# Attention with partitions as (key offset, head), column-tiled folds and v re-laid through DRAM, in a fused adaLN block

## The chip, the cores and the metric

The kernel runs on one core of one Trainium2 chip. The metric is the device time of one execution in microseconds (us). Engine names are those of the profile: PE is TensorE (matmul), PEld its weight loads, DVE VectorE, ACT ScalarE, POOL GpSimd, SP the engine whose queue issues nearly all the DMAs.

## The reference

One transformer block over 2048 rows of 512 columns: LayerNorm with modulation, sliding dilated attention, a residual, LayerNorm with modulation, a gated FFN, a residual. All in bf16.

```python
def _A_ref(x, wqkv, wo):                     # H = 32 heads of Dh = 16
    W, dil = (8, 2)                          # 8 keys per query: the positions s, s-2, ..., s-14
    qkv = ((x @ wqkv).reshape(B, S, 3, H, Dh)).transpose(2, 0, 3, 1, 4)
    ...
    logits = jnp.einsum('bhsd,bhswd->bhsw', q, kg) * scale      # masked where s - 2w < 0
    attn = _softmax(logits, axis=-1)
    o = jnp.einsum('bhsw,bhswd->bhsd', attn, vg)
    return o.transpose(0, 2, 1, 3).reshape(B, S, D) @ wo

def _B_ref(x, w_gate, w_up, w_down):         # Df = 1792
    return jnp.einsum('bsf,fd->bsd', _gelu(g) * u, w_down)

h = _layernorm(x) * (1 + ca) + sa            # sa..gb come from silu(c) @ w_mod
x = x + ga * _A_ref(h, A_wqkv, A_wo)
h = _layernorm(x) * (1 + cb) + sb
x = x + gb * _B_ref(h, B_w_gate, B_w_up, B_w_down)
```

## The kernel before

The rows are worked in four groups of 512 (`sg` 0 to 3). `qT`, `kT` and `vT` hold 128 partitions of (head, d4), four slices `j`, and 512 rows in the free dimension, so that a shift by a key offset is a shift in the free dimension. Feature d of a head is 4 d4 + j. `M` sums the four partitions of a head (column-tiled: four key offsets side by side in 32 PSUM partitions each). The softmax runs with rows on partitions, so there are transposes into it and out of it. P is then broadcast to the (head, d4) partitions through DRAM, and the sum over key offsets is done by PE, by multiplying with the identity and accumulating.

```python
def emit_attention(sg):
    qT, kT, vT = qkv_tiles[sg]
    for wg in range(2):
        LTp = psB.tile([P, SG], F32, name="LTp", tag="mm")
        # four products pq = qT * kT shifted by 2w, each 128x2048, on DVE   (cut)
        for j in range(4):
            for w4 in range(4):
                nc.tensor.matmul(LTp[32 * w4:32 * w4 + 32, :], lhsT=M[:], rhs=pqs[w4][:, j, :],
                                 start=(j == 0), stop=(j == 3), tile_position=(0, 32 * w4))
        nc.scalar.activation(out=LT[:, wg, :], in_=LTp[:], func=ACT.Identity, scale=DH ** -0.5)
    # LT -> transposes LNp -> max, subtract, Exp, sum, reciprocal, product -> transposes PTp -> PT   (cut)
    scr = dram.tile([P, 2, SG], BF16, name="scr")
    nc.sync.dma_start(out=scr[:], in_=PT[:])
    for w in range(W):
        wg, w4 = divmod(w, 4)
        pbc = pbcpool.tile([P, SG], BF16, name="pbc")
        src = bass.AP(scr.tensor, scr.offset + w4 * 32 * (2 * SG) + wg * SG, [[2 * SG, 32], [0, 4], [1, SG]])
        nc.sync.dma_start(out=pbc[:], in_=src)
    for jp in range(2):
        for w in range(W):
            pv = pvpool.tile([P, 2, SG], BF16, name="pv")
            nc.vector.tensor_tensor(out=pv[:], in0=_ap(pbcs[w][:], [[0, 2], [1, SG]]),
                                    in1=vT[:, 2 * jp:2 * jp + 2, 16 - 2 * w:16 - 2 * w + SG], op=ALU.mult)
            for i in range(2):
                nc.tensor.matmul(o_ps[i][:], lhsT=ident[:], rhs=pv[:, i, :], start=(w == 0), stop=(w == W - 1))
    # oT, x1 = x + oT @ (ga wo), LayerNorm 2 -> h2T   (cut)
...
for sg in range(NSG):
    emit_attention(sg)
    if sg == 0:
        emit_qkv(1); emit_ln1(2); emit_qkv(2); emit_ln1(3)
    elif sg == 1:
        emit_qkv(3)
    if sg >= 1:
        emit_ffn(sg - 1)
emit_ffn(NSG - 1, last=True)
```

## Time and profile before

| | before |
|---|---|
| time, median of the runs beside the changed kernel (range) | 306.0 us (305.72 to 306.5) |
| span of the profiled run, mean granted clock | 305.3 us, 0.993 |
| first FFN matmul of group 0 (g_ps) | 85.20 us |
| first LTp matmul of attention(2) | 143.90 us |
| first LTp matmul of attention(3) | 204.96 us (61.06 later) |
| from there to the end | 100.3 us |

The marks of the table are starts in PE's timeline. They cut the span into a front, one steady period (attention of one group woven with the FFN of the group before), and the rest.

From the profile's page of the kernel before: busy time, the 40 slices, and the chain of waits. Then two of its groups, in the form "line, engine, operation, tiles, shapes, count | busy us, mean ns of one | idle time before it".

```profile
PE 268.9 (88%) x1421; PEld 124.7 (41%) x1448; DVE 187.9 (62%) x344; ACT 150.5 (49%) x250; POOL 11.5 (4%) x21
...
PE   0699976899997999899968899899689998999995
PEclk9999999999999999999999999999979999999999
DMA  5999940401000401001000401110004000100001
...
PE 56%; DVE 10%; ACT 7%; issue 3%; DMA 2%; SPq 1%; POOL 1%; POOLq 0%; ACTq 0%; DVEq 0%
...
L308 DVE TENSOR_TENSOR pv<-pbc,vT 128x1024 bf16<-128x1024 bf16 x64 | 42.0, 689 | 4.1 <-DMA pbc<-scr 1.6
L248 DVE TENSOR_TENSOR pq<-qT,kT 128x2048 bf16<-128x2048 bf16 x32 | 37.7, 1217 | 3.7 <-ACT kT L230 3.0
```

The reader sees PE at 9 in most slices from the ninth on (61 us; a slice is 7.6 us), and at 56% of the chain: from about 60 us the time is PE's. The clock stands at full from 17.9 us on; before that the trace has no clock event, and the 9s of the first slices stand there for want of one. The pv products wait little (4.1 us in all, 1.6 of it for pbc).

From PE's timeline of the kernel before, in attention(2) ("start, us, engine line, tiles, count, idle before and what ended it"):

```profile
143.90 1.25 PE L252 MATMUL LTp<-pq,Mph 128*32 128x512 bf16 x17
...
157.42 1.02 PE L350 MATMUL u_ps<-h2T,Wu 128*128 128x512 bf16 x4 [1.55 <-ACT gl L353]
...
171.09 0.38 PE L311 MATMUL o_ps_1671<-pv,ident 128*128 128x512 bf16 x1
171.31 0.38 PE L346 MATMUL g_ps<-h2T,Wg 128*128 128x512 bf16 x1
```

The first line is where attention(2) begins. The next has one of the gaps that belong to the Exp and Gelu table loads on ACT (four loads of 1.28 us between 153.54 and 161.08). The last two show that a full matmul takes 0.216 us of PE's stream: read the distance of the starts, since the modelled 0.38 us overlaps.

### The profile page before, as it was taken

The page shows a single profiled execution, that of the slowest core. Times are in us where ns is not written, and L with a number is a line of the kernel's source. Part 1 is how long each engine was busy: PE and PEld are TensorE (multiplying, and loading weights), DVE is VectorE, ACT ScalarE, POOL GpSimd, SP SyncE. Part 2 cuts the span into 40 slices and gives each one's busy share as a digit, 9 for nine tenths or more (in the row PEclk, how much of TensorE's full clock was granted, in tenths as well). Part 3 has the DMA queues.
Part 4 walks back from the last instruction along what each step waited for, and adds up shares of the span by engine and source line. Part 5 has one row for each costly group of instructions (what it writes and reads, how often), then busy time and mean ns, then how long its engine had stood idle before and what let it go on. Part 6 is the DMA issues. An engine that isn't in the chain of part 4 may idle for free.

```text
span 305.3 us, 3861 instructions
## 1 busy us (share of the span) xinstructions
PE 268.9 (88%) x1421; PEld 124.7 (41%) x1448; DVE 187.9 (62%) x344; ACT 150.5 (49%) x250; POOL 11.5 (4%) x21
## 2 busy tenths in 40 slices
PE   0699976899997999899968899899689998999995
PEld 0445444444453444444323344443244444444442
DVE  4449889899887587522985597426456973222221
ACT  1258577436487543630597433305974343066600
POOL 1110100100200000100000000100000001000000
PEclk9999999999999999999999999999979999999999
DMA  5999940401000401001000401110004000100001
GB/s 175 364 401 344 333 124 34 137 0 54 17 2 0 151 22 38 33 17 37 17 1 34 141 0 53 34 37 17 0 34 140 0 17 19 37 16 2 0 33 35
DMA packets 19154, 22.53 MB, mean 74 GB/s; under 512 B 1856, under 2 KB 16960, under 8 KB 19136
## 3 DMA queue, kind: packets, MB, share of 16 engines
q1 hardware_dynamic: 19136, 22.29, 21.3%
q8 instruction: 11, 0.18, 0.2%
q14 instruction: 7, 0.06, 0.1%
HBM read 19.14 MB, written 3.15 MB: 73 GB/s over the span
## 4 chain that ended last, share of the span: by engine, by line
PE 56%; DVE 10%; ACT 7%; issue 3%; DMA 2%; SPq 1%; POOL 1%; POOLq 0%; ACTq 0%; DVEq 0%
PE u_ps L350 11%; PE y_ps L370 10%; PE g_ps L346 6%; PE qkv_ps L225 5%; PE y_psb L370 4%; PE g_psq L346 4%; PE LTp L252 3%; DVE x1b L326 2%; DVE st L109 2%; PE hTp L128 2%; ACT L276 2%; DMA pbc<-scr 1%; ACT ub L355 1%; DVE ssum L279 1%; PE x_ps L324 1%
## 5 line engine op out<-in xcount | busy, mean ns | idle before, releaser
L350 PE MATMUL u_ps<-h2T,Wu 128*128 128x512 bf16 x220 | 61.2, 383 | 6.5 <-ACT gl L353 6.2
L225 PE MATMUL qkv_ps<-hT,wqkv 128*128 128x512 bf16 x188 | 48.5, 393 | 4.5 <-DMA wqkv<-in_A_wqkv_dram 1.4
L357 DVE TENSOR_TENSOR hht<-gl,ub 128x512 bf16<-128x512 bf16 x56 | 23.4, 421 | 47.1 <-ACT ub L355 47.1
L346 PE MATMUL g_ps<-h2T,Wg 128*128 128x512 bf16 x161 | 47.4, 382 | 3.1 <-ACT ub L355 2.8
L355 ACT CAST ub<-u_ps 128x512 bf16<-128x512 f32 x56 | 32.8, 586 | 25.2 <-PE u_ps L350 25.0
L308 DVE TENSOR_TENSOR pv<-pbc,vT 128x1024 bf16<-128x1024 bf16 x64 | 42.0, 689 | 4.1 <-DMA pbc<-scr 1.6
L248 DVE TENSOR_TENSOR pq<-qT,kT 128x2048 bf16<-128x2048 bf16 x32 | 37.7, 1217 | 3.7 <-ACT kT L230 3.0
L353 ACT ACTIVATE gl<-g_ps 128x512 bf16<-128x512 f32 x42 | 25.3, 603 | 28.8 <-PE g_ps L346 28.1
L370 PE MATMUL y_ps<-WdP,hht 128*128 128x512 bf16 x164 | 37.6, 379 | 0.2
L350 PEld LDWEIGHTS <-Wu 128*128 128x128 bf16 x224 | 21.6, 98 | 32.9 <-issue 9.4
L346 PEld LDWEIGHTS <-Wg 128*128 128x128 bf16 x224 | 21.7, 98 | 28.4 <-issue 5.2
L225 PEld LDWEIGHTS <-wqkv 128*128 128x128 bf16 x192 | 21.3, 116 | 25.9 <-issue 8.2
L370 PEld LDWEIGHTS <-hht 128*128 128x128 bf16 x224 | 21.7, 98 | 24.8
L373 DVE TENSOR_TENSOR ot<-y_ps,x1b 128x512 bf16<-128x512 f32 x12 | 8.3, 692 | 25.4 <-PE y_ps L370 23.1
L311 PEld LDWEIGHTS <-ident 128*128 128x128 bf16 x128 | 12.3, 96 | 20.7 <-issue 9.9
L113 POOL TENSOR_TENSOR rstd<-rstd,neghalf 128x4 f32<-128x4 f32 x8 | 9.8, 1228 | 241.5 <-DVE rstd L112 241.5
L135 ACT ACTIVATE h2T<-hTp,modT,scl 128x512 bf16<-128x512 bf16 x16 | 11.6, 778 | 11.3 <-PE hTp L128 11.3
L254 ACT ACTIVATE LT<-LTp 128x512 f32<-128x512 f32 x8 | 4.8, 601 | 22.3 <-PE LTp L252 22.3
L324 PE MATMUL x_ps<-woP,oT 128*128 128x512 bf16 x63 | 15.5, 378 | 0.2
L346 PE MATMUL g_psq<-h2T,Wg 128*128 128x512 bf16 x55 | 14.3, 379 | 0.1
L228 ACT CAST qT<-qkv_ps 128x512 bf16<-128x512 f32 x16 | 9.4, 586 | 9.1 <-PE qkv_ps L225 9.0
L252 PE MATMUL LTp<-pq,Mph 128*32 128x512 bf16 x128 | 13.4, 383 | 0.0
(118 smaller groups left out, 275.1 us busy)
## 6 DMA issues: line engine op xcount, KB each, us to landing
pbc<-scr SPq DMA_DIRECT2D x32, 128.0 KB, 2.5
wm<-in_w_mod_dram SPq DMA_DIRECT2D x6, 512.0 KB, 6.6
x_sg<-in_A_x_dram SPq DMA_DIRECT2D x4, 512.0 KB, 4.1
xr<-in_A_x_dram SPq DMA_DIRECT2D x16, 128.0 KB, 2.0
out_dram<-ot SPq DMA_DIRECT2D x16, 128.0 KB, 1.7
Wg<-in_B_w_gate_dram SPq DMA_DIRECT2D x1, 1792.0 KB, 12.1
Wu<-in_B_w_up_dram SPq DMA_DIRECT2D x1, 1792.0 KB, 9.7
WdP<-in_B_w_down_dram SPq DMA_DIRECT2D x1, 1792.0 KB, 9.8
```

The source lines that it names most:

```text
L225: nc.tensor.matmul(ps[:], lhsT=wqkv[:, dt, blk * D + j:(blk + 1) * D:4], rhs=hT[:, dt, :], start=(dt == 0), stop=(dt == DT - 1))
L248: nc.vector.tensor_tensor(out=pq[:], in0=qT[:], in1=kT[:, :, 16 - 2 * w:16 - 2 * w + SG], op=ALU.mult)
L252: nc.tensor.matmul(LTp[32 * w4:32 * w4 + 32, :], lhsT=M[:], rhs=pqs[w4][:, j, :], start=(j == 0), stop=(j == 3), tile_position=(0, 32 * w4))
L308: nc.vector.tensor_tensor(out=pv[:], in0=_ap(pbcs[w][:], [[0, 2], [1, SG]]), in1=vT[:, 2 * jp:2 * jp + 2, 16 - 2 * w:16 - 2 * w + SG], op= ...
L311: nc.tensor.matmul(o_ps[i][:], lhsT=ident[:], rhs=pv[:, i, :], start=(w == 0), stop=(w == W - 1))
L324: nc.tensor.matmul(x1_ps[:], lhsT=oT[:, j, c4 * P:(c4 + 1) * P], rhs=woP[:, j, :], start=(j == 0), stop=(j == 3))
L346: nc.tensor.matmul(g_ps[:], lhsT=Wg[:, dt, ft * P:(ft + 1) * P], rhs=h2T[:, dt, :], start=(dt == 0), stop=(dt == DT - 1))
L350: nc.tensor.matmul(u_ps[:], lhsT=Wu[:, dt, ft * P:(ft + 1) * P], rhs=h2T[:, dt, :], start=(dt == 0), stop=(dt == DT - 1))
L353: nc.scalar.activation(out=gl[:], in_=g_ps[:], func=ACT.Gelu_apprx_tanh)
L355: nc.scalar.copy(out=ub[:], in_=u_ps[:])
L357: nc.vector.tensor_tensor(out=hht[:], in0=gl[:], in1=ub[:], op=ALU.mult)
L370: nc.tensor.matmul(y_ps[:], lhsT=hh[ft][:, c4 * P:(c4 + 1) * P], rhs=WdP[:, ft, :], start=(ft == 0), stop=(ft == FT - 1))
```

## The change

Its intent: spend fewer PE columns and less DVE time on attention. The partitions become (key offset r, head). The logits stay there, so no transposes are needed: the maximum is three DVE operations and a matmul that subtracts it in PSUM, the sums are column-tiled matmuls. The fold of pv over the four key offsets in the partitions becomes a 32-column matmul, four of them side by side (`tile_position`), instead of full matmuls with the identity. For that, v must lie in (r, head) partitions, each r shifted by two rows; it is written to DRAM and read back in that layout. x stays in SBUF instead of being read again, 14 dummy matmuls run at the start to wake PE's clock, and loads are issued in order of use. The `emit_` calls keep their order in the source, but the scheduled order of instructions changes: qkv(2) begins at about 50 us in the trace of the kernel before, and behind the start of FFN(0) in the changed kernel.

```diff
+        order = [(b, j) for j in range(4) for b in range(2)] + [(2, j) for j in range(4)]
         ...
+        scr = dram.tile([P, 4, HALO + SG], BF16, name="scr")
+        nc.sync.dma_start(out=scr[:], in_=vT[:])
+        row = HALO + SG
+        for j in range(4):
+            vRj = vrpool.tile([P, 4, VW], BF16, name="vR")                 # VW = 520
+            src = bass.AP(scr.tensor, scr.offset + 2 + j * row, [[2, 4], [16 * row, H], [4 * row, 4], [1, VW]])
+            nc.sync.dma_start(out=vRj[:], in_=src)
     ... (softmax: LNp, PTp, PT, pbc go; m3, NB, ss, rB come; cut)
-            for w in range(W):
-                nc.vector.tensor_tensor(out=pv[:], in0=_ap(pbcs[w][:], [[0, 2], [1, SG]]), in1=vT[...], op=ALU.mult)
-                for i in range(2):
-                    nc.tensor.matmul(o_ps[i][:], lhsT=ident[:], rhs=pv[:, i, :], start=(w == 0), stop=(w == W - 1))
+            for wg in range(2):
+                nc.vector.tensor_tensor(out=pv[:], in0=_ap(e[:, wg, :], [[0, 4], [1, SG]]),
+                                        in1=vR[j][:, :, 8 - 8 * wg:8 - 8 * wg + SG], op=ALU.mult)
+                for d4 in range(4):
+                    nc.tensor.matmul(o_ps[32 * d4:32 * d4 + 32, :], lhsT=F1[:], rhs=pv[:, d4, :],
+                                     start=(wg == 0), stop=(wg == 1), tile_position=(0, 32 * d4))
     ...
-    nc.sync.dma_start(out=woP[:], in_=A_wo.rearrange("(p j) n -> p j n", j=4))
+    nc.sync.dma_start(out=woP[:], in_=bass.AP(A_wo.tensor, A_wo.offset, [[4 * D, 4], [16 * D, H], [D, 4], [1, D]]))
+    for i in range(14):
+        nc.tensor.matmul(wps[:], lhsT=warm[:, 0:P], rhs=warm[:], start=True, stop=True)
```

## The prediction

> **What bounds it now.** TensorE, by its in-order stream, from about 60 us on. The page gives PE 268.9 us busy of 305.3, DVE 187.9, ACT 150.5. PE holds 56% of the chain of waits. The timeline shows full-size matmuls back to back every 0.216 us; counting by that spacing, real PE work is about 253 us. The rest: head 13.2 us to the first qkv matmul, about ten qkv matmuls at 0.43 us instead of 0.216 (13.2 to 17.8 us), tail 3.6 us after the last matmul, and PE idle in the middle. The timeline from one attention to the next (143.97 to 205.03) has 61 us for 52 us of PE work; its gaps are waits for ScalarE near the two Exp table loads (1.55, 1.39, 0.89), for P (0.5), for the P broadcast through DRAM (1.46) and for LN2 (1.14).
>
> **What the change does.**
> PE: o_ps falls from 128 full matmuls (27.6 us) to 128 32-column ones, four side by side. The LTp runs show 17 of these in 1.19 us and 13 in 0.97, so 0.054 each plus a fixed cost; a lone LTp costs 0.42 in all instead of 0.216. I read a fixed 0.3 to 0.36 us per group, which agrees with the Trainium skill, "TensorEngine Tiling (Array Packing)", Key Properties: changing the tiling mode drains TensorE. The new order alternates four folds with three or four FFN matmuls, so a group costs an estimated 0.58 us, not 0.22: 32 o_ps groups 14 to 18 us, and more LTp groups too. Gone: LNp and PTp transposes (5.5 us). New: max subtraction, sums, 1/sum broadcast, about 5 us. Net PE work down only about 8 to 12 us.
> DVE: mx, LT, ssum, rinv, e products (27.2 us) become three max, rinv, two copies and one product (about 15); pv 42.0 to 39 us; pq unchanged, 1.22 us each.
> ACT: PT copy (4.0) and one of two Exp table pairs per attention (2.6) go.
> DMA: P's round trip (2.0 plus 4.4 us in the chain) leaves the critical path; v's, four times larger, starts right after qkv and should be hidden.
> Head: 14 dummy matmuls should make the first qkv matmuls run at 0.216: 2 us.
>
> **How much is critical.** In the two steady periods I expect 55 to 57 us instead of 61: about 10 us. In the front the gain is nearly lost: attention(0) ends some 15 us earlier, but the new order puts LN1(2), LN1(3), qkv(2), qkv(3) after FFN(0) has begun, so PE has nothing to do while the DVE chain softmax, 8 pv, x1, LN2 runs (about 35 to 64 us, some 15 us idle). FFN(0) starts near 65 instead of 82 us. Front gain: 2 to 5 us.
>
> **Prediction: 290 us, 280 to 300 (8 in 10); faster by over 2%: 0.88, within 2%: 0.11, slower: 0.01.**
>
> **What shows it.** First qkv matmuls 0.216 us apart by 13 us; o_ps groups of four taking 0.5 to 0.6 us between FFN matmuls (0.3 would refute the mode-switch cost); pv 1.22 us; no wait on vR; PE share low between 35 and 65 us; distance between the LT runs of attention(2) and (3) 55 to 57 us; one Exp table load per attention.
>
> **What would make it wrong.** Switch cost hidden by queued weights: 280 or lower. pq with the overlapping key window or pv falling to half rate (2.2 us): slower, near 306. vR landing late beside Wu and WdP. Longer PE gaps in the front.

## The result

All ratios below are the mean time of one kernel's runs over that of the other's runs of the same rounds, so they are not quite the ratio of the medians quoted beside them. Executions over 1.5% slower than the fastest of the same kernel are left out of the means.

| | before | after |
|---|---|---|
| time, median (range) | 306.0 us (305.72 to 306.5) | 303.73 us (303.34 to 304.89) |
| ratio, 95% interval | | 0.9926 (0.9904 to 0.9947) |
| span of the profiled run, mean granted clock | 305.3 us, 0.993 | 302.1 us, 0.932 |
| first g_ps of FFN(0) | 85.20 | 83.09 |
| first LT matmul of attention(2) | 143.90 | 158.19 (14.3 later) |
| to the first LT matmul of attention(3) | 61.06 | 51.88 (9.2 less) |
| from there to the end | 100.3 | 92.0 (8.3 less) |

The kernel is 0.7% faster, within 2%; the forecast was 5%. The three stages add up: 14.3 - 9.2 - 8.3 = -3.2 us, the difference of the two spans. The two later stages gained more than was forecast. The front lost 14.3 us where a gain of 2 to 5 was forecast. The page of the changed kernel, in the same order:

```profile
PE 264.5 (88%) x1476; PEld 113.3 (38%) x1476; DVE 172.9 (57%) x305; ACT 142.0 (47%) x238; POOL 18.1 (6%) x41
...
PE   7696986128399999998999899899989989999995
PEclk9699899555669999999999999999999999999999
DMA  7999422694222122231220012100000000100000
...
PE 65%; DMA 12%; DVE 11%; SPq 4%; ACT 3%; POOL 2%; issue 1%; POOLq 0%; DVEq 0%; ACTq 0%
...
L318 DVE TENSOR_TENSOR pv<-e,vR 128x2048 bf16<-128x2048 bf16 x32 | 37.0, 1219 | 11.7 <-DMA vR<-scr 11.6
L273 DVE TENSOR_TENSOR pq<-qT,kT 128x2048 bf16<-128x2048 bf16 x32 | 37.9, 1212 | 6.4 <-PE LT_471 L276 6.4
```

Three things are new. PE's row falls to 1, 2, 8, 3 in slices 8 to 11 (53 to 83 us), with PEclk at 5 and 6 there. DMA holds 12% of the chain. The pv group now waits 11.6 us for vR, though one pv product takes the 1.22 us that was forecast.

DVE's timeline of the changed kernel in attention(0):

```profile
46.24 2.36 DVE L318 TENSOR_TENSOR pv<-e,vR 128x2048 bf16<-128x2048 bf16 x2
50.25 2.40 DVE L318 TENSOR_TENSOR pv<-e,vR 128x2048 bf16<-128x2048 bf16 x2 [1.65 <-DMA vR<-scr]
56.53 2.36 DVE L318 TENSOR_TENSOR pv<-e,vR 128x2048 bf16<-128x2048 bf16 x2 [3.88 <-DMA vR<-scr]
64.94 2.36 DVE L318 TENSOR_TENSOR pv<-e,vR 128x2048 bf16<-128x2048 bf16 x2 [6.05 <-DMA vR<-scr]
```

Four pairs of products take 9.5 us; they spread over 21 us, because each of the last three pairs waits for its load of v (1.65, 3.88 and 6.05 us). Next, the DMA issues on SP's queue, and the two pieces of the chain of waits that lie ahead of those products:

```profile
34.70 15.51 SPq L258 DMA_DIRECT2D vR<-scr  x4
50.25 5.68 SPq L389 DMA_DIRECT2D Wu<-in_B_w_up_dram  x1
55.97 1.34 SPq L390 DMA_DIRECT2D WdP<-in_B_w_down_dram  x1
```

```profile
25.36 9.28 DMA scr<-vT
...
44.51 20.31 DMA vR<-scr
```

The write of v to DRAM takes 9.3 us. SP then spends 15.5 us on issuing four loads; Wu and WdP, the FFN's weights, stand behind them in the queue. The last piece of the chain lasts 20.3 us, until the last of the four loads lands at 64.8 us. What the DMA engines did meanwhile is in the windows (columns: window and its length, busy us and count of PE, PEld, DVE, ACT, POOL, then granted clock, busy share of the 16 DMA engines, GB/s):

```profile
40.00:45.00 5.00, 3.90 (x30) 2.05 (x29) 1.49 (x4) 3.92 (x6) 0.00 (x0) 1.00 0.27 87
45.00:50.00 5.00, 4.74 (x26) 1.98 (x25) 3.57 (x3) 3.06 (x6) 0.23 (x1) 1.00 0.27 92
50.00:55.00 5.00, 0.80 (x8) 0.20 (x7) 2.40 (x2) 1.00 (x2) 1.04 (x1) 0.87 0.27 92
55.00:60.00 5.00, 1.23 (x8) 0.23 (x8) 2.36 (x2) 0.39 (x1) 0.00 (x0) 0.50 0.76 190
60.00:65.00 5.00, 0.00 (x0) 0.00 (x0) 0.06 (x1) 0.20 (x1) 0.00 (x0) 0.50 1.03 266
```

From 35 to 55 us the share is 0.27 and stays there: 4.3 engines' worth of 16, moving about 90 GB/s. Wu cannot be the competitor, since its issue began at 50.25 us. After that the share goes to 1.03. So the loads are slow because they do not use the engines, and not because the engines are busy. The single DMA packets in the kept trace show the same: the 1040-byte pieces of vR take 48 ns each, with 4.3 packets in flight on average from 34.7 to 56 us. The first three loads' pieces are through at 54.75 us, before the share rises. The fourth load's take 8.9 us instead of 5.8: some 3 us of the last wait of 6.05 come from sharing with Wu and WdP, by this estimate.

Last, PE's timeline of the changed kernel: the start of attention(2), against 143.90 before, and the fold in the steady part:

```profile
158.19 0.40 PE L276 MATMUL LT_1543<-pq,Mph 128*32 128x512 bf16 x4
...
177.43 0.59 PE L346 MATMUL g_ps<-h2T,Wg 128*128 128x512 bf16 x2
177.96 0.40 PE L321 MATMUL o_ps<-pv,F_157 128*32 128x512 bf16 x4
178.29 0.60 PE L346 MATMUL g_ps<-h2T,Wg 128*128 128x512 bf16 x2
```

Two g_ps matmuls should take 2 x 0.216 = 0.43 us; the group of four folds starts 0.53 us after them and takes 0.33 us itself. A group thus costs 0.43 us, not the 0.58 that was forecast (the median of the 15 such groups between FFN matmuls after 100 us is 0.43 too, the longest 0.48).

### The profile page after: what moved, and what is told of

It is laid out like the page before. It is cut to its first block, busy times and chain, and to the rows that moved or that the text cites. A ratio compares the mean times of both kernels' runs of the same rounds, so it can differ in the third digit from the quotient of the medians.

```text
span 302.1 us, 3849 instructions
## 1 busy us (share of the span) xinstructions
PE 264.5 (88%) x1476; PEld 113.3 (38%) x1476; DVE 172.9 (57%) x305; ACT 142.0 (47%) x238; POOL 18.1 (6%) x41
## 4 chain that ended last, share of the span: by engine, by line
PE 65%; DMA 12%; DVE 11%; SPq 4%; ACT 3%; POOL 2%; issue 1%; POOLq 0%; DVEq 0%; ACTq 0%
PE u_ps L350 13%; PE y_ps L368 12%; PE qkv_ps L246 10%; PE g_ps L346 9%; DMA vR<-scr 7%; PE y_psb L368 4%; PE g_psq L346 4%; PE x_ps L329 4%; SPq L258 3%; PE o_ps L321 3%; DMA scr<-vT 3%; DVE st L183 3%; PE hTp L200 3%; DVE x_sg L331 2%; DMA wm<-in_w_mod_dram 2%; POOL rstd L187 2%
## 5 line engine op out<-in xcount | busy, mean ns | idle before, releaser
L350 PE MATMUL u_ps<-h2T,Wu 128*128 128x512 bf16 x224 | 62.6, 383 | 0.0
L346 PE MATMUL g_ps<-h2T,Wg 128*128 128x512 bf16 x168 | 49.3, 387 | 0.9 <-ACT h2T L207 0.9
L318 DVE TENSOR_TENSOR pv<-e,vR 128x2048 bf16<-128x2048 bf16 x32 | 37.0, 1219 | 11.7 <-DMA vR<-scr 11.6
L350 PEld LDWEIGHTS <-Wu 128*128 128x128 bf16 x224 | 20.7, 98 | 25.5 <-issue 5.1
L321 PE MATMUL o_ps<-pv,F_157 128*32 128x512 bf16 x128 | 13.7, 416 | 14.5 <-DVE pv L318 14.4
L371 DVE TENSOR_TENSOR ot<-y_ps,x_sg 128x512 bf16<-128x512 f32 x12 | 8.3, 691 | 26.2 <-PE y_ps L368 21.6
L183 DVE BATCH_NORM_STATS2 st<-x_sg 128x6 f32<-128x512 bf16 x32 | 20.9, 672 | 3.8 <-DMA x_sg<-in_A_x_dram 3.8
L187 POOL TENSOR_TENSOR rstd<-rstd,neghalf 128x4 f32<-128x4 f32 x8 | 10.6, 1330 | 187.6 <-DVE rstd L186 187.6
L323 ACT CAST oT<-o_ps 128x512 bf16<-128x512 f32 x16 | 9.4, 586 | 23.2 <-PE o_ps L321 23.2
L329 PE MATMUL x_ps<-woP,oT 128*128 128x512 bf16 x64 | 18.8, 434 | 0.7 <-ACT oT L323 0.7
L207 ACT ACTIVATE h2T<-hTp,modT,scl 128x512 bf16<-128x512 bf16 x16 | 11.6, 787 | 14.7 <-PE hTp L200 14.6
L353 ACT ACTIVATE gl<-g_psq 128x512 bf16<-128x512 f32 x14 | 8.4, 597 | 14.6 <-PE g_psq L346 14.6
```

The lines of the kernel that those rows point to most:

```text
L183: nc.vector.bn_stats(out=st[:, c4, :], in_=xt[:, c4, :])
L318: nc.vector.tensor_tensor(out=pv[:], in0=_ap(e[:, wg, :], [[0, 4], [1, SG]]), in1=vR[j][:, :, 8 - 8 * wg:8 - 8 * wg + SG], op=ALU.mult)
L321: nc.tensor.matmul(o_ps[32 * d4:32 * d4 + 32, :], lhsT=F1[:], rhs=pv[:, d4, :], start=(wg == 0), stop=(wg == 1), tile_position=(0, 32 * d4))
L329: nc.tensor.matmul(x1_ps[:], lhsT=oT[:, j, c4 * P:(c4 + 1) * P], rhs=woP[:, j, :], start=(j == 0), stop=(j == 3))
L346: nc.tensor.matmul(g_ps[:], lhsT=Wg[:, dt, ft * P:(ft + 1) * P], rhs=h2T[:, dt, :], start=(dt == 0), stop=(dt == DT - 1))
L350: nc.tensor.matmul(u_ps[:], lhsT=Wu[:, dt, ft * P:(ft + 1) * P], rhs=h2T[:, dt, :], start=(dt == 0), stop=(dt == DT - 1))
```

## The experiments

Two theories were put against each other. Theory A: vR's source pattern has the key offset, a dimension of four, outermost, so each load runs on only four of the 16 DMA engines. The Trainium skill, "DMA: Bandwidth & Descriptors", section "Why a DMA increments its semaphore by 16 and not by 1", says that the number of engines is the largest k up to 16 that divides the slowest dimension (not of size 1) of both access patterns; the share of 0.27 agrees with k = 4. Theory B: the loads are slow for another reason (their size, 1040-byte pieces, the wait for the write to DRAM before them, or Wu and WdP beside them), or the front is lost to PE's clock or to the column-tiled matmuls. All kernels gave correct results. The changed kernel itself was not run again in the later batches, whose runs of the kernel before have medians of 306.44 to 307.87 us instead of 306.0. Differences from 303.73 below are therefore between batches; by the ratios they would be 1 to 1.5 us larger.

### Split vR's load so that heads are outermost (e1_vr16)

```diff
-            src = bass.AP(scr.tensor, scr.offset + 2 + j * row, [[2, 4], [16 * row, H], [4 * row, 4], [1, VW]])
-            nc.sync.dma_start(out=vRj[:], in_=src)
+            for r in range(4):
+                src = bass.AP(scr.tensor, scr.offset + 2 + j * row + 2 * r, [[16 * row, H], [4 * row, 4], [1, VW]])
+                nc.sync.dma_start(out=vRj[32 * r:32 * r + 32], in_=src)
```

> Only the load of vR changes: each of the 4 loads per group of rows is issued as 4 loads of 32 partitions, so that the outermost dimension of the read is 32 (heads) instead of 4 (key offsets). Same bytes, same pieces of 1040 B, same place in the queue. Theory A (a read whose outermost dimension is 4 runs on only 4 of the 16 DMA engines: share 0.27, 92 GB/s, 5.8 us per 520 KB): the waits of pv on vR fall from 11.6 us to under 2, the first g_ps starts at 65 to 70 us instead of 83, the DMA share is near 1 while vR lands, and the time is 284 to 290 us instead of 303.7. Rival B (small scattered pieces of 1040 B, or a DRAM write followed by a read, are slow in themselves) and rival C (vR is late because Wu and WdP compete with it): pv still waits 8 us or more and the time stays over 298 us. Rival D (the gain is eaten by the tiling-mode switches on TensorE or by the colder clock for its own reasons): vR lands early and the time still stays over 298 us.

Measured: 290.61 us (290.21 to 291.41), ratio to the kernel before 0.9461 (0.9421 to 0.9501). No pv product waits for vR. The first g_ps comes at 70.78 us instead of 83.09, attention(2) at 145.30 instead of 158.19. One of its windows:

```profile
40.00:45.00 5.00, 3.88 (x25) 1.71 (x25) 1.48 (x3) 4.28 (x7) 0.00 (x0) 1.00 0.69 195
```

The share goes from 0.27 to 0.69, and the same bytes flow twice as fast. In the packets, a piece of 1040 bytes still takes 47 ns, but 11 are in flight on average from 40 to 46 us. The 16 loads are issued in 10.85 us, 0.68 each, and their pieces move in 11.2 us, so probably the issuing bounds them now; no run tests that. About 13 us came back. The edit changes two things, the outermost dimension and the number of loads; the control below parts them. The time is just above the 284 to 290 expected.

### The control: split it as finely, with the key offset still outermost (e2_vr_split_k4)

```diff
+            for d4 in range(4):
+                src = bass.AP(scr.tensor, scr.offset + 2 + j * row + 4 * d4 * row, [[2, 4], [16 * row, H], [1, VW]])
+                nc.sync.dma_start(out=vRj[:, d4, :], in_=src)
```

> Control for the run before it: vR also loaded by 16 smaller loads instead of 4, of the same pieces, but split over the depth group, so that each still has the key offset (4) outermost. Theory A: nothing gained, pv waits 10 to 14 us for vR, DMA share 0.27 while vR lands, time 301 to 307 us. If splitting into more and smaller transfers is what helps (pipelining, or shorter queues), it lands with the run before it, under 292 us.

Measured: 301.33 us (300.83 to 302.33), ratio 0.981 (0.9767 to 0.9853), inside what theory A expected. The order of instructions on PE, DVE, ACT and SP is that of the changed kernel, but for the number of loads (in e1_vr16 the scheduler also moved some instructions on PE, DVE and ACT); the number and size of the loads are those of e1_vr16.

```profile
40.00:45.00 5.00, 3.88 (x25) 1.72 (x25) 1.48 (x3) 4.27 (x7) 0.00 (x0) 1.00 0.27 90
45.00:50.00 5.00, 4.95 (x33) 2.46 (x32) 4.31 (x4) 2.63 (x6) 0.24 (x1) 1.00 0.27 90
```

The share is 0.27 again (4.3 packets in flight), and pv waits 8.9 us for vR, a little less than the 10 to 14 expected. So it is the outermost dimension and not the size or number of the loads: 10.7 us between e2 and e1, which ran in the same batch. Splitting by itself is worth some 2 us (303.73 against 301.33, between batches); finer overlap with the products would explain it, but that was not tested.

### Split the wo load alone, and both loads (e3_wo16, e4_both16)

wo's new load also has a dimension of four outermost, `[[4*D,4],[16*D,H],[D,4],[1,D]]`.

```diff
+    for d4 in range(4):
+        nc.sync.dma_start(out=woP[32 * d4:32 * d4 + 32],
+                          in_=bass.AP(A_wo.tensor, A_wo.offset + 4 * d4 * D, [[16 * D, H], [D, 4], [1, D]]))
```

> Only the load of woP changes, the other load whose outermost dimension is 4: split in 4 loads of 32 partitions. Theory A says that it clogs 4 of the 16 engines, and that the loads behind it (wm block 3, Wg) finish late: the first LT matmul, held by wm block 3 until 29.05 us, should start near 26 us, and about 3 us be gained in all if vR moves up as much (299 to 302 us). If the load of woP has slack: 303 to 305 us. It may not be read as cleanly as the others, as the scheduler then also puts Wg behind vR in the queue.

Measured: 300.44 to 301.62 us in three runs (a fourth, 311.8, was slow and is left out), ratio 0.9791 (0.9743 to 0.984). vR's first load is issued at 29.6 us instead of 34.70, and pv still waits 11.5 us for vR. The kernel starts its v loads earlier and is held by them as before. The scheduler also moved Wg's load behind vR's here, so this run does not show how the gain divides between the two. The write of v and the start of its loads are what moved: 3.2 us from the issue of the one to the issue of the other (26.42 to 29.61), against 9.3 (25.36 to 34.70).

> Both loads split over heads. Theory A: the gain of vR alone plus up to 3 us: 281 to 288 us; TensorE still has an idle stretch before the first g_ps (softmax, pv, x1, LN2 on DVE with nothing else to do), of about 10 us, and with it a stretch at half clock. Rivals B, C: over 298 us.

Measured: 288.79 us (287.33 to 289.73), 0.8 us above what was expected, ratio 0.9387 (0.9331 to 0.9442); first g_ps at 69.08, attention(2) at 142.97, then 52.4 us to attention(3) and 92.2 to the end. DVE's timeline of it shows the eight products of attention(0) in one run, without a wait:

```profile
44.49 9.21 DVE L319 TENSOR_TENSOR pv<-e,vR 128x2048 bf16<-128x2048 bf16 x8
```

The two patterns together cost the changed kernel 15 us (303.73 against 288.79); in this the split into more loads and Wg's place behind vR, which moved here too, are included. What is left of the front's gain is 0.9 us (142.97 against 143.90). e9_both16_again is the same kernel in a later batch, as the base for the runs of that batch (the expectation speaks of another chip; the record lists chip 1 for both, so only the batch is known to differ):

> The kernel with both split loads once more, as the base of the three runs that share its chip (the first run of it was on another chip, with the kernel before 0.5% slower there). 287.5 to 289.5 us.

Measured: 288.74 us (287.48 to 289.9), ratio 0.9424 (0.9381 to 0.9468); attention(2) at 141.13.

### The changed kernel without its 14 dummy matmuls (e5_after_nowarm)

```diff
-    for i in range(14):
-        nc.tensor.matmul(wps[:], lhsT=warm[:, 0:P], rhs=warm[:], start=True, stop=True)
```

> The kernel after without its 14 dummy matmuls. The prediction counted 2 us for them. The trace of after shows the first qkv matmuls at half clock all the same (record 0.50 between 10 and 15 us; 48 matmuls in 12.7 us, as before), so the theory now is that the clock falls back between the dummies' end at 6.7 us and the first qkv matmul at 12 us, and that they are worth nothing: 303.5 to 304.5 us, within 0.5 us of after. If they do help, it is slower by 1 to 2 us.

Measured: 304.13 us (303.46 to 307.51), ratio 0.9934 (0.9892 to 0.9976), against 0.9926 for the changed kernel: the dummies are worth nothing that five rounds can see. PE's timeline of the changed kernel, and its windows, show why:

```profile
1.29 5.45 PE L154 MATMUL warm_ps<-warm 128*128 128x512 bf16 x14 [1.29 <-DVE neghalf L113]
...
11.96 8.39 PE L246 MATMUL qkv_ps<-hT,wqkv 128*128 128x512 bf16 x28 [1.30 <-DVE hT L204]
```

```profile
8.00:10.00 2.00, 1.39 (x28) 1.39 (x29) 1.31 (x4) 0.24 (x2) 1.03 (x4) 0.83 1.08 380
14.00:16.00 2.00, 2.00 (x6) 0.64 (x5) 2.00 (x6) 0.73 (x2) 0.00 (x0) 0.50 1.09 386
```

The dummies end at about 6.7 us; the first eleven of them start 0.43 us apart, the last ones 0.216, so they do wake the clock, at 5.9 us. Five microseconds of small matmuls and gaps follow, and the clock's record falls to 0.50 at 9.31 us. qkv starts at half rate all the same: its matmuls start 0.43 us apart until 16.0 us. The 48 matmuls of qkv(0) end at 24.7 us. In e5 they begin at 12.39 and end at 24.2. The Trainium skill, "TensorE: Matmul & The Clock Gate", section "What's actually happening", gives an idle window of about 3.4 us after which the clock halves. The record of this trace agrees in the length: full clock from 5.90 to 9.31 us, 3.41 us. But PE was not wholly idle in it (the last dummies and 32 matmuls of one column fall into it), so what counts as idle isn't shown here. In the kernel before, the trace has no clock event ahead of 17.90 us; its qkv matmuls start 0.43 us apart until 17.87 and 0.216 after. The dummies warmed the clock too early.

### The fold without column tiling (e6_fullfold)

e4_both16, with the four 32-column folds replaced by four full matmuls with zero-padded weights that accumulate in one PSUM tile.

```diff
-                    nc.tensor.matmul(o_ps[32 * d4:32 * d4 + 32, :], lhsT=F1[:], rhs=pv[:, d4, :],
-                                     start=(wg == 0), stop=(wg == 1), tile_position=(0, 32 * d4))
+                    nc.tensor.matmul(o_ps[:], lhsT=FD[:, d4, :], rhs=pv[:, d4, :],
+                                     start=(wg == 0 and d4 == 0), stop=(wg == 1 and d4 == 3))
```

> On top of both split loads: the fold of pv into o_ps by full 128x128 matmuls with zero-padded weights (as many as the change has, 128, each 0.216 us, no change of tiling mode) in place of four 32-column ones side by side. The trace of after shows a group of four at 0.33 us plus about 0.1 us before it (0.43), against 4 x 0.216 = 0.86 for full ones, so the column tiling saves 0.43 us a group, 14 us of TensorE time in 32 groups. If TensorE is the limit there: 10 to 14 us slower than the kernel with both loads split (299 to 303 us). If the pace of pv on DVE (1.22 us a group) sets the time: under 4 us slower.

Measured: 302.22 us (301.67 to 303.06), ratio 0.9857 (0.9816 to 0.9898). PE's timeline of it:

```profile
167.95 1.02 PE L326 MATMUL o_ps<-pv,FD 128*128 128x512 bf16 x4
168.81 0.38 PE L355 MATMUL u_ps<-h2T,Wu 128*128 128x512 bf16 x1
```

A group of four takes 0.86 us, against 0.43 for the tiled one. Over 32 groups that is 32 x 0.43 = 13.8 us; the medians differ by 13.4. By stages, attention(2) starts 5.4 us later than in e4 (1.2 of it already at the first qkv matmul), the period to attention(3) is 3.6 us longer and the rest 4.1. So each attention from the second on pays about 4 us, and the first, where PE waits anyway, next to nothing: the close match of 13.8 and 13.4 is partly luck. Where PE is the limit, its saved time is the kernel's saved time. It also says that without column tiling the rest of the change is worth about 4 us (302.22 against 306.44 for the kernel before in the runs beside it), the mended loads included.

### Work for PE in the front (e7_filler)

e4_both16 with LN1(2) emitted right after LN1(1), so that qkv(2) runs before FFN(0), into the time in which PE waits for attention(0).

```diff
     emit_ln1(1)
+    emit_ln1(2)
     ...
-            emit_ln1(2)
             emit_qkv(2)
```

> On top of both split loads: LN1 of the third group of rows is emitted before attention(0), so that the 48 matmuls of qkv(2) (10.4 us) stand in TensorE's order before FFN(0) begins. Theory: TensorE sits idle or at half clock from 48 to 72 us for want of ready work; with qkv(2) there, the first g_ps starts 2 to 5 us later (LN1 costs DVE 4 us), but with 10.4 us of work done and the clock kept up: 279 to 284 us against about 288.8. If DVE's chain is the limit also later: no gain.

Measured: 285.20 us (284.16 to 285.26), ratio 0.9291 (0.9259 to 0.9324), about 1 us above what was expected. g_ps begins later than in e4_both16 (75.89), but attention(2) comes 3.5 us earlier (139.52; the profile of e9, the same kernel as e4, has it at 141.13, so profiles differ by up to 2 us here, while the medians differ by 3.6). Together with e11 below it is the fastest kernel: 7% below the kernel before by the ratio, and 6% below the changed kernel by the medians.

### The half clock in the front (e8_keepwarm, e12_keepwarm_again, e10_after_keepwarm, e11_filler_keepwarm)

PE's clock record stands at 0.50 from 53.7 to 87.8 us in the changed kernel, but for 3.4 us after 74.2, and for shorter times in e4_both16. Dummy matmuls with zero weights were put on pv and x1 in attention(0), to keep PE busy while it waits. The edit shown is that of e8 and e12; e11 has only dummies after x1 (26), on e7_filler, and e10 has 3, 16 or 24 after the folds and 18 after x1, on the changed kernel.

```diff
+                if sg == 0 and j > 0:
+                    for i in range(3):
+                        nc.tensor.matmul(wps[:], lhsT=warm[:, 0:P], rhs=pv[:, i, :], start=True, stop=True)
     ...
+            if sg == 0 and c4 == 3:
+                for _ in range(22):
+                    nc.tensor.matmul(wps[:], lhsT=warm[:, 0:P], rhs=xt[:, c4, :], start=True, stop=True)
```

> On top of both split loads: dummy matmuls (zero weights on pv and x1, so that they come at the right time) in the idle gaps of attention(0), 3 after each fold and 22 before LN2's transposes. They do no work; only the clock can gain. Theory: the stretch at half clock (15 x_ps in 5.45 us, first FFN matmuls at 0.43 until 72.5 us) costs 4 to 5 us; with the clock kept up the time is 283 to 286 us against about 288.8. If the half clock only falls into time that DVE's chain would hold anyway: within 1.5 us of 288.8.

> The dummies with both split loads once more, now on the chip of their base: the profiles of the two first runs put the start of attention(2) at 139.5 us with the dummies and 143.0 us without, so 2.5 to 3.5 us faster than the base. If the half clock is hidden, within 1 us of it.

Measured: 286.92 us (285.79 to 288.18), ratio 0.9357 (0.9319 to 0.9394), and in the batch of e9_both16_again 286.93 (286.39 to 288.33), ratio 0.9367 (0.933 to 0.9403), against 288.74 for e9. The mean clock rises from 0.964 to 0.988 and the time falls by 1.8 us (1.5 in the means), with overlapping intervals. That lies between the two outcomes that e8 and e12 set out: neither hidden nor the 2.5 us and more that were expected. The half clock is worth some 2 us once the loads are mended; PE in the front waits for DVE's chain for part of that time anyway.

> Filler (LN1 of the third group early, so qkv(2) before FFN(0)) and both split loads, and 26 dummy matmuls after x1(0), where that version was still at half clock from 70 to 82 us. About 12 FFN matmuls and 8 transposes at half rate there are 3 us: 282.5 to 284.5 us against 285.2 without. If hidden: 284.5 to 286 us.

Measured: 284.89 us (284.22 to 286.15), ratio 0.9299 (0.9262 to 0.9335): nothing over e7_filler (0.9291).

> The kernel after, loads unchanged, with dummy matmuls (zero weights, on pv and x1) in TensorE's idle stretches of attention(0): 3 or 16 or 24 after each fold and 18 after x1. What the late vR costs beyond the wait itself: theory, the half clock between 52 and 88 us costs 4 to 6 us of the 303.7 (16 x_ps at 0.43 instead of 0.216 are 3.4 us, the first FFN matmuls 1 to 2 us), so 298 to 300.5 us. If the half clock is hidden behind DVE's chain: 302.5 to 304.5 us.

Measured: 314.43 us (313.27 to 314.79), ratio 1.0249 (1.021 to 1.0288). This experiment failed to isolate the clock. DVE's timeline of it:

```profile
65.52 2.36 DVE L318 TENSOR_TENSOR pv<-e,vR 128x2048 bf16<-128x2048 bf16 x2 [6.15 <-PE warm_ps L325]
...
74.15 4.79 DVE L366 TENSOR_TENSOR WdP<-WdP,gbB 128x512 bf16<-128x512 bf16 x14 [5.13 <-DMA WdP<-in_B_w_down_dram]
```

With the dummies in it, the program's order on DVE came out different: the 14 products of WdP with gb, which wait for WdP's load, stand ahead of the x1 additions, and PE's next x_ps waited 12.2 us for those. The pv products also waited for dummies that still read their buffers. So no run measures what the half clock costs inside the changed kernel itself. The kept traces give an estimate for a part of it: from the last pair of pv products to the first g_ps it is 18.2 us there (64.94 to 83.09), with half clock for 14.7 of it, 17.7 us in e4 (10.6 at half clock), and 15.9 us in e8 and e12 at full clock. By this estimate, from profiles that differ in their loads too, the half clock costs about 2.3 us up to the first g_ps; what it costs from there to 87.8 us, where it ends, stays open.

## Why the prediction was wrong

**The step that failed** is, in its own words: "v's, four times larger, starts right after qkv and should be hidden". The write did start right after qkv (25.36 us), but it took 9.3 us, and only then, at 34.70, could the loads start. The prediction has no term for this trip and none for the number of engines; it knows only the size. An estimate shows what it needed: four loads of 520 KB are 2.1 MB, at 90 GB/s 24 us, for products that want them all within 9.5 us from 46 us on. The rule that gives the four engines stands in the Trainium skill; I did not look up what the new pattern's outermost dimension would do. "No wait on vR" was refuted: 11.6 us. e1 against e2 shows the cause (10.7 us), and e4 its whole size, 15 us with wo's pattern. The term that it broke is "FFN(0) starts near 65": it started at 83.09, and with both loads mended at 69.08 (e4) or 66.6 (e9).

**A right symptom with the smaller cause.** The prediction listed "vR landing late beside Wu and WdP". vR did land late, but the first two waits fell at a share of 0.27, while the engines had room. Wu and WdP can at most have delayed the last of the four loads, which landed at a share of 1.03, by some 3 us (the estimate above). That they met it at all follows from its lateness: in e1 the loads' pieces are through at 47.5 us.

**The front.** "Front gain: 2 to 5 us" became a loss of 14.3. With the two loads mended the front gains 0.9 (e4) or 2.8 us (e9). So even with the loads mended the front's gain is "nearly lost", as was argued: in e4 FFN(0) starts 16 us earlier than before (69.08 against 85.20), and attention(2) hardly earlier. That the new order is the reason is shown only in part: e7, which puts qkv(2) back ahead of FFN(0), got 3.5 us back.

**The steady part.** "55 to 57 us instead of 61" was the right mechanism with a size too large for the group: "an estimated 0.58 us", measured 0.43. The period is 51.9, and the two later stages gain 17.5 us where about 10 were forecast. The switch costs something: a group of four would be 0.22 us by the spacing of 0.054 within one run of LTp matmuls. The drain when the tiling mode changes, which the Trainium skill states ("TensorEngine Tiling (Array Packing)", Key Properties), would account for the other 0.2 us a group, though no run separates it from other costs of the switch; 0.3 to 0.36 had been read into it.

**The sum.** The front was 16 to 19 us worse than forecast, the later stages 7.5 us better. The difference, 9 to 12 us, and the head that was counted separately (2 us) give 11 to 14 us; the miss was 303.73 - 290 = 13.7. That e4 and e9 stand at 288.8, next to the forecast of 290, is partly luck: two errors of the remaining sum, a group too dear and a front gain too large, nearly cancel.

**The head.** "14 dummy matmuls should make the first qkv matmuls run at 0.216: 2 us" was wrong: they start at half rate, and e5 shows no worth. qkv starts 1.2 us earlier (11.96 against 13.20), but e5 without the dummies starts at 12.39, and the profiles of e1 to e4, with the same dummies, at 12.2 to 13.2: no gain can be read from this.

**Right as forecast:** pv at 1.22 us, pq unchanged, one Exp table load per attention (4 in all; before there were 5, two each in attention(2) and (3), one in attention(0), and none in attention(1), which ran before FFN(0) had begun), and PE bound in the later stages (e6).

**Not tested:** x kept in SBUF, and the new softmax, each by itself; together with all that is left they are about 4 us in e6. The share of the half clock in the changed kernel (e10 failed; about 2.3 us of it by the estimate above).

## What to carry to other kernels

Before counting a DMA as hidden, read its access patterns and not only its bytes: the outermost dimension decides how many DMA engines work, and a share that stays flat at 4 of 16 in the windows, with no other load in flight, is its signature. When a change moves a large transfer into a front where everything waits in one chain, cost its landing time against the moment of first use, and what stands behind it in its queue. Make a control that splits as finely and keeps the suspected property, as e2 did here; without it, e1's gain could have been put down wholly to smaller loads, which account for some 2 of its 13 us.

## What the Trainium skill lacked or had wrong

- "DMA: Bandwidth & Descriptors" has the rule for the number of engines, but no measured rate of a transfer on fewer than 16 of them, and nothing on what it does to the issuing queue. Here k = 4 gave about 90 GB/s with pieces of 1040 bytes, 22 GB/s per engine, and SP was held for 15.5 us by four such loads (19.9 us when split into 16 with the same outermost dimension, 10.9 us when split into 16 with heads outermost).
- The same page, "Rules for kernel authors", says of two transfers to disjoint partition halves "Don't bother", because both halves use all 16 engines. The reason did not hold here: four loads of 32 partitions each were 10.7 us faster (290.61 against 301.33) than a split as fine that kept the dimension of four outermost. The row on using all 16 engines in the same table has the remedy, to put a large dimension outermost; the first row does not point to it.
- "TensorEngine Tiling (Array Packing)" states the drain at a change of mode without a figure. A group of four 32-column matmuls between full ones cost 0.43 us here, where the spacing within a long run would give 0.22.
- No page has this point on reading the clock: the windows of a trace show 1.00 where there is no clock event yet. In the kernel before they read 1.00 from 12 to 18 us, while the qkv matmuls from 13.2 us on start every 0.43 us until 17.87; the first event is at 17.90. The spacing of matmuls is the safer reading there.
